# Turned products of an inverse transform in DRAM: laid out by rows, written in pieces, read as one run per partition

## The chip, the cores and the metric

The kernel runs on one core of a Trainium2 chip. The core has five engines that run their own instruction streams side by side: TensorE (matmuls; PE in the profile, with its weight loads as PEld), VectorE (DVE), ScalarE (ACT), GpSimd (POOL) and SyncE (SP), which here only issues DMAs. 16 DMA engines move data between DRAM and the on-chip memory SBUF, whose first dimension is 128 partitions. Matmul results go to PSUM and are copied out by ScalarE or VectorE. The metric is the time of one execution on the device, in microseconds (us); lower is better.

## The reference

An input x of 2048 steps by 512 channels goes through two branches, which a gate mixes:

```python
x = A_u
g = _sigmoid((x * gate_w).sum(-1, keepdims=True))
a = _A_ref(x, ...)      # state space model as a long convolution
b = _B_ref(x, ...)      # linear attention, 32 heads of 16
return g * a + (1 - g) * b
```

The change touches the end of branch A. There a kernel K of 2048 taps is made for each channel, and the convolution is done by Fourier transforms of length 4096:

```python
K = jnp.einsum("dn,dnl,dn->dl", Cc, P, dB).real
Kf = rfft(pad(K));  Uf = rfft(pad(u))
Yf = Uf * Kf
y = irfft(Yf)[:L] + u * Dskip
```

## The kernel before

The program is one long list of nodes (class `Plan`), each with its engine; a string `ORDER`, written out by hand, sets the order in which all are issued, and so each engine's order and SyncE's queue. An engine runs its instructions strictly in that order. DMAs share eight lanes (`"ln": 8`), so a ninth waits for an earlier one to land.

The first part (to about 100 us) makes tables, transforms u and writes its spectrum to DRAM (`XUd`). The second part works through 16 units of 32 channels: `kgen` makes the taps K of a unit (products `A` and `R` on VectorE at L1097, L1108, L1115, L1119, matmuls `kps` at L179) and their first transform step (`psA`, L186). When the channels of a group are ready, `transform` finishes the convolution for them. The groups are: Q = 0, 1 and 2 with nd = 128 channels each (units 0 to 3, 4 to 7, 8 to 11), and in Q = 3 one group of nd = 64 (units 12, 13), one of nd = 32 (unit 14) and a last one of nd = 32 (unit 15). Branch B's attention runs between these on the same engines.

Inside `transform`, for `ns` frequency rows r at a time (8, 16 or 32 for nd = 128, 64 or 32):

- `load` (L1182, for Q = 3 L1184) brings the spectrum of u from DRAM into a tile XUX, of which there are three; it is a pair of DMAs of 256 KB. `psB` (L192) makes the spectrum of K, a copy takes it to `XK`, and VectorE multiplies the two: tile `t` (L1229; for the nd = 32 groups L1232, in two halves).
- `fi` (L1261) multiplies with the table TI as weights: the first step of the inverse transform. Its 128 outputs stand on the partitions, numbered by t (32), h (2) and a (2); the free dimension holds (r, d), d the channel. ScalarE copies them to a tile `Zr` (two buffers).
- The second step contracts over a and r and needs them on the partitions, with t on the free dimension. The products are turned through DRAM: `fw` (L1274) writes each `Zr` to a DRAM tensor `Zd`, four times for nd = 128, twice for nd = 64, once for nd = 32; `fr` (L1283) reads `Zd` back into a tile ZT of 128 partitions, 64 partitions (one h, called `th`) with each of two DMAs. A reading waits until all writings of its group have landed.
- `py` (L1339) does the second step from ZT with the table TJ: `psy`. For nd = 128 it comes in two instalments, the first with the first reading's half, the second with the other's. `ou` (L1361, L1364) scales with the gate and stores the result, which is then written to the output.

The last group (unit 15, `far` false) does not go through DRAM: `iz` (L1295) takes `t` as weights and TI as the moving operand, one t half and one a at a time.

ZT shares one buffer (tag `ax`) with the attention's factors `ax`. These go through DRAM too: `aw` (L895) writes them to `apd` as 64 KB, and `ar` (L902) reads them back as four DMAs of 256 KB. Each reading repeats 8 rows of DRAM for 16 partitions each: its DRAM side is `.unsqueeze(1).to_broadcast([8, 16, 1024])` against 128 partitions of SBUF. VectorE multiplies with them at L909.

The table TI itself is made at about 7 us by two sines on ScalarE and three small operations of VectorE (L299 to L301).

Of the kernel before, what the change touches and what calls it, by code (L numbers as in the profile page):

```python
# [13 lines left out]
BF16 = mybir.dt.bfloat16  # L14
# [1041 lines left out]
def plan_conv(P, nc, g, psum, r):  # L1056

    fc, act, at, xT = g.fc, g.act, g.at, g.xT
# [6 lines left out]
    def evict2(name, get, deps, ps):  # L1065
        out = []
        for k in range(2):
            out.append(P.add(("ACT", "DVE"), name, lambda k=k: P.copy(*get(k)), [ps] + deps[k] + out, drop=(["psum"] if k else [])))
        return out
# [119 lines left out]
    def transform(XA, ready, Q, off, nd, far, Ls, last, co=0, free=True, split=False):  # L1189

        F = Bag()
        ng, ns, nj, nt = nd // 2, 1024 // nd, min(16, 1024 // nd) if far else 8, min(32, 2048 // nd)
# [4 lines left out]
        ov = g.out2d[:, 128 * (Q - pair) + lo:128 * Q + off + nd].rearrange("(q j c) d -> c q j d", q=32, j=16, c=4)  # L1197
        bS = xT[:, :, Q, :]
        if far:
            F.Zd = g.dram.tile([32, 4, 32, nd], BF16, name=f"Zd{Q}_{off}")  # L1200
        tn, zn, rn, wn = [], [], [], []
        for r0 in range(0, 32, ns):
            box = Bag()
# [44 lines left out]
            x = evict2("XK", xk, [[], []], b) if split else [evict("XK", xk, [b])]  # L1248
# [8 lines left out]
            def fi(box=box):  # L1257
                box.ps = psum([128, 2, 512], "psz")
                for hb in range(2):
                    for k in range(2):  # L1260
                        nc.tensor.matmul(box.ps[:, hb, :], lhsT=fc.TI[:, k].rearrange("p t h a -> p (t h a)"), rhs=box.t[:, k, 512 * hb:512 * hb + 512],  # L1261
                                         start=(k == 0), stop=(k == 1))
                box.t = None

# [6 lines left out]
                return o, i  # L1271

            def fw(r0=r0, box=box):
                nc.sync.dma_start(out=F.Zd[:, :, r0:r0 + ns, :].rearrange("t x r d -> (t x) r d"), in_=box.Z[:])  # L1274
                box.Z = None
            z = P.add("PE", "psz", fi, [tn[-1]] + ([z] if r0 else []), take=[psq, "Zr"], drop=(["r8"] if (r0 + ns) % nt == 0 else []), rw=("TI", ""))
            zn.append(evict("Zr", fe, [z] + zn[-1:]))
            wn.append(P.dma("zw", 0.45, 2.0, fw, [zn[-1]], drop=["Zr"], move=0.9))

        def fr(th):  # L1280
            if th == 0:
                F.Z = g.fpool.tile([128, 4096], BF16, name="ZT", tag="ax", bufs=g.P.k["ax"])[:, 0:32 * nd].rearrange("p (t d) -> p t d", d=nd)
            nc.sync.dma_start(out=F.Z[64 * th:64 * th + 64], in_=F.Zd[:, 2 * th:2 * th + 2].rearrange("t x r d -> (x r) t d"))  # L1283
        for th in range(2 if far else 0):
            rn.append(P.dma("zr", 0.6, 2.0, lambda th=th: fr(th), wn + [n.issue for n in rn[-1:]], take=(["ax"] if th == 0 else []), move=max(1.2, 2.8 * nd / 128 + 0.1)))
        box = Bag()
# [25 lines left out]
        for j0 in range(0, 16, nj):  # L1312
            box = Bag()
# [81 lines left out]
    for h in range(6):  # L1395
        for u in (2 * h, 2 * h + 1):
            if u in g.PHASES and u:
                phase(range(u, g.PHASES[u]))
        if h % 2 == 0:
            XA = Bag()  # L1400
            XA.nd, XA.off, XA.drop, done = 128, 0, True, []
        done = done + kgen((2 * h, 2 * h + 1), XA, h % 2 == 0)
        if h % 2:
            transform(XA, done, h // 2, 0, 128, True, [load(h // 2, p) for p in range(4)], False)
# [7 lines left out]
    for k, (units, far) in enumerate(g.LAST):  # L1412
        XA = Bag()
        XA.nd, XA.off, XA.first = 32 * len(units), 32 * (units[0] - 12), first
        XA.drop = units[-1] == 15
        done = kgen(units, XA, True, units in g.SPLIT)
        first = XA.first
        end = units[-1] == 15
        off = 32 * (units[0] - 12)
        transform(XA, done, 3, off, XA.nd, far, L[off // 64 * 2:off // 64 * 2 + 2], end, off % 64, units[-1] % 2 == 1, units in g.SPLIT)  # L1420


def full_kernel(tc, A_u, A_A_re, A_A_im, A_B_re, A_B_im, A_C_re, A_C_im, A_log_dt, A_Dskip,
                B_x, B_wqkv, B_w_phi, B_wo, gate_w, out):
    nc = tc.nc
# [3 lines left out]
    def pool(ctx, name, bufs=1, **kw):  # L1429
        return ctx.enter_context(tc.tile_pool(name=name, bufs=bufs, reuse_waits="tile", **kw))  # L1430
    with ExitStack() as ctx:
        g, fc, at = Bag(), Bag(), Bag()
# [6 lines left out]
        persist = pool(ctx, "persist")  # L1439
# [6 lines left out]
        g.zrow = persist.tile([128, 4, 128], F32, name="zrow")  # L1446
        fc.W1 = persist.tile([128, 2, 32, 4], BF16, name="W1")
        fc.TB = persist.tile([128, 97, 64], BF16, name="TB")
        fc.TI = persist.tile([128, 2, 32, 2, 2], BF16, name="TI")
        fc.TJ = persist.tile([128, 64, 32], BF16, name="TJ")  # L1450
        g.CX = [persist.tile([128, 3072], BF16, name=f"Ctab{h}") for h in range(2)]
        g.C = [c[:].rearrange("p (o a c) -> p o a c", o=3, a=4) for c in g.CX]
# [111 lines left out]
        r = keys_and_spectrum(P, nc, g, psum)  # L1564
# [7 lines left out]
@with_exitstack  # L1572
def kernel(
    ctx: ExitStack,
    tc: tile.TileContext,
    A_u: bass.AP,
    A_A_re: bass.AP,
    A_A_im: bass.AP,
    A_B_re: bass.AP,
    A_B_im: bass.AP,  # L1580
    A_C_re: bass.AP,
    A_C_im: bass.AP,
    A_log_dt: bass.AP,
    A_Dskip: bass.AP,
    B_x: bass.AP,
    B_wqkv: bass.AP,
    B_w_phi: bass.AP,
    B_wo: bass.AP,
    gate_w: bass.AP,
    out: bass.AP,  # L1590
):
    full_kernel(tc, A_u, A_A_re, A_A_im, A_B_re, A_B_im, A_C_re, A_C_im, A_log_dt, A_Dskip,
                B_x, B_wqkv, B_w_phi, B_wo, gate_w, out)
# [30 lines left out]
```

## Time and profile before

| what | value |
|---|---|
| time, median of 3 runs (lowest, highest) | 264.5 us (263.61, 264.85) |
| the profiled execution's own time | 264.49 us |
| its span, first to last instruction | 262.7 us |
| VectorE busy, ScalarE busy | 231.0 us, 221.1 us |
| TensorE busy, mean granted clock | 195.3 us, 0.927 |
| packets of SyncE's DMA queue, as a share of 16 engines' span | 54.5% |
| bytes moved by all DMAs | 35.93 MB |

The span is 1.8 us shorter than the time of the same execution. Busy times are sums over one engine; they overlap with those of the others. In the timeline a row gives the start in us, the duration, engine, line, operation, tiles (out<-in), shape and count; in square brackets stands how long the engine had been idle and what released it. Rows of SyncE (SPq) are the issuing alone: the data moves afterwards. A row of a DMA queue (q1 is SyncE's) gives packets, MB and the share of the time of 16 engines in the window that was asked for.

The kernel's chain of work that ended last consists of VectorE for 35%, ScalarE 27%, TensorE 18%, DMA 8%.

### The profile page before, as it was taken

Reading aid. Unit: us, or ns where it says so; the run is one execution under the profiler, and the core shown is the slowest. Engines: PE = TensorE matmul, PEld = TensorE weight load, DVE = VectorE, ACT = ScalarE, POOL = GpSimd, SP = SyncE. Lnnn points to the kernel's source line nnn. Section 1 sums busy time; section 2 is a strip of 40 time slices with the busy share of each in tenths; the row PEclk is TensorE's granted clock in tenths of the full one; section 3 lists DMA queues with packets and bytes.
Section 4 is the critical chain, followed back from the end, with each engine's and each line's share of the span. In section 5 each row is a group of like instructions: output and inputs, shape, how many; then the busy total and the mean of one; then the engine's idle time right before and its main releaser. Section 6 shows DMA issues by size and latency. Waiting matters only on the chain.

```text
span 262.7 us, 10078 instructions
## 1 busy us (share of the span) xinstructions
PE 195.3 (74%) x4512; PEld 132.4 (50%) x4512; DVE 231.0 (88%) x314; ACT 221.1 (84%) x305; POOL 11.7 (4%) x22
## 2 busy tenths in 40 slices
PE   0386899999945569888468656989978598998750
PEld 0275665755633234355346244575765376774630
DVE  6799799898799998999999999989999999975440
ACT  7976998888899999999999998999999997765000
POOL 4750000000000000000000000000000000000000
PEclk9997999999999597999899999899999999999655
DMA  6799000352630576602240536258945697979784
GB/s 196 140 192 214 4 4 0 99 154 62 202 95 24 178 220 182 206 4 86 101 150 15 162 130 201 67 152 160 226 148 199 175 195 229 166 214 161 176 102 82
DMA packets 67547, 35.93 MB, mean 137 GB/s; under 512 B 46000, under 2 KB 62000, under 8 KB 67504
## 3 DMA queue, kind: packets, MB, share of 16 engines
q1 hardware_dynamic: 66448, 35.16, 54.5%
q8 instruction: 35, 0.57, 1.0%
q10 hardware_dynamic: 1056, 0.13, 0.3%
q14 instruction: 8, 0.07, 0.1%
HBM read 22.17 MB, written 13.11 MB: 134 GB/s over the span
## 4 chain that ended last, share of the span: by engine, by line
DVE 35%; ACT 27%; PE 18%; DMA 8%; issue 8%; SPq 1%; DVEq 0%; ACTq 0%
DVE A L1097 7%; DMA XUX<-XUd 4%; DVE t L1229 3%; PE pk L705 3%; ACT Eq L68 3%; ACT XA L145 2%; ACT xst L145 2%; ACT E L68 2%; DMA ax<-apd 2%; DVE XAu L147 2%; DVE R L1119 2%; ACT cs L68 2%; DVE R L1115 2%; ACT Zr L145 2%; DMA pz<-pt 2%
## 5 line engine op out<-in xcount | busy, mean ns | idle before, releaser
L1097 DVE TENSOR_TENSOR A<-Ctab,Dtab 128x2048 bf16<-128x2048 bf16 x32 | 38.7, 1219 | 0.2
L68 ACT ACTIVATE cs<-args 128x1024 bf16<-128x1024 f32 x32 | 30.9, 1063 | 0.0
L179 PE MATMUL kps<-R,A 128*32 128x64 bf16 x1536 | 18.1, 204 | 8.0 <-DVE A L1097 1.8
L179 PEld LDWEIGHTS <-A 128*32 128x32 bf16 x1536 | 16.3, 118 | 12.0 <-issue 5.6
L1115 DVE TENSOR_TENSOR R<-E,cs 128x2048 bf16<-128x2048 bf16 x16 | 19.5, 1220 | 1.6 <-ACT E L68 1.5
L1119 DVE TENSOR_TENSOR R<-E,cs 128x2048 bf16<-128x2048 bf16 x16 | 19.5, 1217 | 0.0
L68 ACT ACTIVATE Ek<-pk 128x512 bf16<-128x512 f32 x32 | 16.7, 602 | 2.5 <-PE pk L705 2.5
L1261 PE MATMUL psz<-t,TI 128*128 128x512 bf16 x60 | 15.6, 388 | 2.8 <-DVE t L1229 1.2
L1229 DVE TENSOR_TENSOR t<-XUX,XK 128x2048 bf16<-128x2048 bf16 x14 | 17.0, 1218 | 0.4 <-ACT XK L145 0.4
L145 ACT CAST XA<-psA 128x1024 bf16<-128x1024 f32 x15 | 15.1, 1042 | 2.6 <-PE psA L186 2.6
L68 ACT ACTIVATE E<-args 128x1024 bf16<-128x1024 f32 x16 | 16.8, 1057 | 0.2 <-PE args L1041 0.2
L145 ACT CAST Zr<-psz 128x1024 bf16<-128x1024 f32 x15 | 15.4, 1027 | 1.6 <-ACT xT L977 0.7
L68 ACT ACTIVATE Eq<-pq 128x512 bf16<-128x512 f32 (+1 forms) x28 | 16.6, 692 | 0.1
L145 ACT CAST XK<-psB 128x1024 bf16<-128x1024 f32 x15 | 15.4, 1035 | 1.6 <-PE psB L192 1.5
L753 PE MATMUL vp<-WW,xT 128*128 128x512 bf16 x64 | 16.7, 395 | 0.0
L839 PE MATMUL pq<-xT,Wqp 128*128 128x512 bf16 x64 | 16.1, 388 | 0.4 <-ACT Eq L68 0.4
L612 PE MATMUL psB<-XAu,TB 64*128 64x128 bf16 x256 | 9.7, 222 | 8.2 <-ACT xst L145 6.4
L705 PE MATMUL pk<-WW,xT 128*128 128x512 bf16 x64 | 15.2, 380 | 0.0
L186 PE MATMUL psA<-W,KD 128*64 128x128 bf16 x256 | 10.0, 221 | 5.3 <-ACT cs L68 3.1
L192 PE MATMUL psB<-XA,TB 128*128 128x128 bf16 (+2 forms) x192 | 10.1, 200 | 4.5 <-ACT XK L145 1.4
L612 PEld LDWEIGHTS <-TB 64*128 64x128 bf16 x256 | 7.8, 97 | 11.0 <-issue 11.0
L65 ACT ACT_TABLE_LOAD x10 | 12.8, 1283 | 0.1
(210 smaller groups left out, 497.2 us busy)
## 6 DMA issues: line engine op xcount, KB each, us to landing
XUX<-XUd SPq DMA_DIRECT2D x32, 256.0 KB, 5.3
XUd<-xst SPq DMA_DIRECT2D x8, 512.0 KB, 3.1
ax<-apd SPq DMA_DIRECT2D x16, 256.0 KB
Zd<-Zr SPq DMA_DIRECT2D x15, 256.0 KB, 2.4
ZT<-Zd SPq DMA_DIRECT2D x6, 512.0 KB
UD<-in_A_u_dram SPq DMA_DIRECT2D x16, 128.0 KB, 4.5
XUd<-xst SPq DMA_DIRECT2D x8, 256.0 KB
wqk<-in_B_wqkv_dram SPq DMA_DIRECT2D x1, 1024.0 KB
```

The lines of the kernel that those rows point to most:

```text
L68: return self.nc.scalar.activation(**kw)
L145: self.nc.scalar.copy(out=o, in_=i)
L179: nc.tensor.matmul(kps[32 * dj:32 * dj + 32, g4, e, :], lhsT=A[:, d // 4, 32 * ka:32 * ka + 32, d % 4], rhs=R[:, kr, d, :], start=(i == 0) ...
L612: nc.tensor.matmul(box.ps[:, c2, sl, :], lhsT=fc.TB[rows, b0:b0 + 2].rearrange("p a b -> p (a b)"), rhs=X.t[rows, k, r0 + sl].rearrange("p ...
L705: nc.tensor.matmul(box.ps[:], lhsT=xT[:, st, kt, :], rhs=g.WW[:, kt, :], start=(kt == 0), stop=(kt == 3))
L753: nc.tensor.matmul(box.ps[:], lhsT=xT[:, st, kt, :], rhs=g.WW[:, 4 + kt, :], start=(kt == 0), stop=(kt == 3))
L839: nc.tensor.matmul(box.ps[:, m - m0, :] if late else box.ps[:], lhsT=g.Wqp[:, kt, 128 * m:128 * m + 128], rhs=xT[:, 4 * b:4 * b + 4, kt, : ...
L1097: nc.vector.tensor_tensor(out=c.A[:, :, 64 * k:64 * k + 64, :].rearrange("p q (x b) l -> p x b q l", b=8), in0=cf.unsqueeze(2).to_broadcas ...
L1115: nc.vector.tensor_tensor(out=c.R[:, :, :, 32:64], in0=t.E[:, 1].unsqueeze(1).to_broadcast([128, 2, 32, 32]), in1=t.cs[:], op=ALU.mult)
L1119: nc.vector.tensor_tensor(out=c.R[:, :, :, 0:32], in0=t.E[:, 0].unsqueeze(1).to_broadcast([128, 2, 32, 32]), in1=t.cs[:, ::-1, :, ::-1], o ...
L1229: nc.vector.tensor_tensor(out=box.t, in0=Ls[r0 // ns].X[:], in1=box.XK[:].unsqueeze(1).to_broadcast([128, 2, 1024]), op=ALU.mult)
L1261: nc.tensor.matmul(box.ps[:, hb, :], lhsT=fc.TI[:, k].rearrange("p t h a -> p (t h a)"), rhs=box.t[:, k, 512 * hb:512 * hb + 512], start=( ...
```

## The change

The order of the products on the partitions becomes (h, a, t) instead of (t, h, a): the tile behind TI is laid out as [k, h, a, t], and `fc.TI` becomes a view of it with the old order of its dimensions, through which it is made and through which L1295 reads it. With x = (h, a), partition 32·x + t now holds what partition 4·t + x held.

For nd = 128 and 64 (`byrow`) `Zd` is now indexed [r, x, t, d] instead of [t, x, r, d]. A writing puts, for each partition, `ns` pieces of nd elements to places 128·nd elements apart (before: one run of 1024 elements). A reading takes for each of 64 partitions one run of 32·nd elements (before: 32 pieces of nd elements). For nd = 32 `Zd` keeps its layout; the writing names its partitions as x, then t, and the reading is unchanged.

| | before: DRAM side | after: DRAM side |
|---|---|---|
| writing, nd = 128 (256 KB) | 128 runs of 2 KB | 128 partitions with 8 pieces of 256 B |
| writing, nd = 64 (256 KB) | 128 runs of 2 KB | 128 partitions with 16 pieces of 128 B |
| writing, nd = 32 (256 KB) | 128 runs of 2 KB, evenly spaced | 4 (x) with 32 (t) runs of 2 KB |
| reading, nd = 128 (512 KB) | 64 evenly spaced rows with 32 pieces of 256 B | 2 (x) with 32 (r) runs of 8 KB |
| reading, nd = 64 (256 KB) | 64 evenly spaced rows with 32 pieces of 128 B | 2 (x) with 32 (r) runs of 4 KB |

In the readings after the change a step of x is 32·nd elements and a step of r is 128·nd.

```diff
         if far:
+            byrow = nd > 32
             F.Zd = g.dram.tile([32, 4, 32, nd], BF16, name=f"Zd{Q}_{off}")
...
-                        nc.tensor.matmul(box.ps[:, hb, :], lhsT=fc.TI[:, k].rearrange("p t h a -> p (t h a)"), rhs=box.t[:, k, 512 * hb:512 * hb + 512],
+                        nc.tensor.matmul(box.ps[:, hb, :], lhsT=fc.TIp[:, k].rearrange("p h a t -> p (h a t)"), rhs=box.t[:, k, 512 * hb:512 * hb + 512],
...
             def fw(r0=r0, box=box):
-                nc.sync.dma_start(out=F.Zd[:, :, r0:r0 + ns, :].rearrange("t x r d -> (t x) r d"), in_=box.Z[:])
+                if byrow:
+                    nc.sync.dma_start(out=F.Zd[r0:r0 + ns].rearrange("r x t d -> (x t) r d"), in_=box.Z[:])
+                else:
+                    nc.sync.dma_start(out=F.Zd[:, :, r0:r0 + ns, :].rearrange("t x r d -> x t (r d)"), in_=box.Z[:].rearrange("p r d -> p (r d)"))
                 box.Z = None
...
-            nc.sync.dma_start(out=F.Z[64 * th:64 * th + 64], in_=F.Zd[:, 2 * th:2 * th + 2].rearrange("t x r d -> (x r) t d"))
+            if byrow:
+                nc.sync.dma_start(out=F.Z[64 * th:64 * th + 64], in_=F.Zd[:, 2 * th:2 * th + 2].rearrange("r x t d -> x r t d"))
+            else:
+                nc.sync.dma_start(out=F.Z[64 * th:64 * th + 64], in_=F.Zd[:, 2 * th:2 * th + 2].rearrange("t x r d -> (x r) t d"))
...
-        fc.TI = persist.tile([128, 2, 32, 2, 2], BF16, name="TI")
+        fc.TIp = persist.tile([128, 2, 2, 2, 32], BF16, name="TI")
+        fc.TI = fc.TIp[:].rearrange("p k h a t -> p k t h a")
```

The order of issue is the same string as before.

## The prediction

> **What bounds the kernel now.** I read the page first (busy shares), then VectorE's and TensorE's timeline around the readings of Zd, SyncE's timeline from 150 us on, and last the packets of three short windows.
>
> ```profile
> PE 195.3 (74%) x4512; PEld 132.4 (50%) x4512; DVE 231.0 (88%) x314; ACT 221.1 (84%) x305; POOL 11.7 (4%) x22
> Zd<-Zr SPq DMA_DIRECT2D x15, 256.0 KB, 2.4
> ```
>
> VectorE works 231.0 of 262.7 us, so until the tail a DMA matters only when it comes so late that VectorE or TensorE stands still. The points where they use what comes from DRAM are these (VectorE and TensorE, in order of time):
>
> ```profile
> 201.78 1.22 DVE L909 TENSOR_TENSOR Eq<-Eq,ax 128x2048 bf16<-128x2048 bf16 x1
> 213.76 0.63 PE L1339 MATMUL psy<-ZT,TJ 64*32 64x128 bf16 x32
> 215.95 1.21 DVE L1364 TENSOR_TENSOR xT<-psy,gT 128x1024 bf16<-128x1024 f32 x1
> 221.72 0.63 PE L1339 MATMUL psy<-ZT,TJ 64*32 64x128 bf16 x32
> 225.09 1.22 DVE L1097 TENSOR_TENSOR A<-Ctab,Dtab 128x2048 bf16<-128x2048 bf16 x1
> 232.97 0.63 PE L1339 MATMUL psy<-ZT,TJ 64*32 64x128 bf16 x32
> 233.65 0.69 DVE L1361 TENSOR_TENSOR xT<-psy,gT 128x512 bf16<-128x512 f32 x1 [0.46 <-PE psy L1339]
> 239.48 0.69 DVE L1232 TENSOR_TENSOR t<-XUX,XK 128x1024 bf16<-128x1024 bf16 x1 [0.73 <-DMA XUX<-XUd]
> 243.88 0.68 PE L1339 MATMUL psy<-ZT,TJ 64*32 64x64 bf16 x64
> 246.34 3.64 PE L1295 MATMUL psz<-TI,t 128*32 128x64 bf16 x128 [1.78 <-DVE t L1232]
> 253.99 0.77 PE L1339 MATMUL psy<-ZT,TJ 64*32 64x32 bf16 x64
> ```
>
> No `psy` waits for ZT by a DMA's name: today the readings are hidden. Only 239.48 waits for a DMA, a load of XUX. And this is SyncE's queue, all on one ring:
>
> ```profile
> 153.10 2.46 SPq L902 DMA_DIRECT2D ax<-apd  x4
> ...
> 174.29 0.63 SPq L1283 DMA_DIRECT2D ZT<-Zd  x1
> 179.27 0.87 SPq L1182 DMA_DIRECT2D XUX<-XUd  x2
> 180.19 0.61 SPq L1283 DMA_DIRECT2D ZT<-Zd  x1
> 182.15 3.03 SPq L1182 DMA_DIRECT2D XUX<-XUd  x2
> 186.06 0.33 SPq L1274 DMA_DIRECT2D Zd<-Zr  x1
> 187.29 0.93 SPq L1182 DMA_DIRECT2D XUX<-XUd  x2
> 188.98 0.33 SPq L1274 DMA_DIRECT2D Zd<-Zr  x1
> 190.47 0.33 SPq L895 DMA_DIRECT2D apd<-apm  x1
> ...
> 195.34 2.51 SPq L902 DMA_DIRECT2D ax<-apd  x4
> ...
> 206.98 0.62 SPq L1283 DMA_DIRECT2D ZT<-Zd  x1
> 210.13 1.62 SPq L1274 DMA_DIRECT2D Zd<-Zr  x2
> 211.79 0.61 SPq L1283 DMA_DIRECT2D ZT<-Zd  x1
> 212.45 2.83 SPq L1184 DMA_DIRECT2D XUX<-XUd  x2
> 217.77 1.91 SPq L1274 DMA_DIRECT2D Zd<-Zr  x2
> 219.77 1.37 SPq L1184 DMA_DIRECT2D XUX<-XUd  x2
> 222.49 2.46 SPq L1283 DMA_DIRECT2D ZT<-Zd  x2
> 230.20 1.73 SPq L1274 DMA_DIRECT2D Zd<-Zr  x2
> 231.98 1.87 SPq L1184 DMA_DIRECT2D XUX<-XUd  x4
> 247.84 2.12 SPq L1283 DMA_DIRECT2D ZT<-Zd  x2
> ```
>
> **How many DMA engines a transfer gets.** The window from 155 to 159 us holds data of the four `ax` readings of 153.10 and little else; beside it stand one of XUX loads with 1 KB rows (148 to 150), one of 256 B writings (59 to 60) and one of 128 B writings (254.5 to 257), each with packets, MB and the share of 16 engines:
>
> ```profile
> q1 hardware_dynamic: 369, 0.71, 50.5%
> XUX<-XUd SPq DMA_DIRECT2D x2, 256.0 KB, 7.0
> ...
> q1 hardware_dynamic: 579, 0.56, 89.5%
> ...
> q1 hardware_dynamic: 819, 0.22, 95.5%
> ...
> q1 hardware_dynamic: 1831, 0.23, 66.8%
> ```
>
> With four transfers outstanding, only 50.5% of 16 engines work: eight. If each `ax` reading had eight engines of its own, two would fill all 16; so all four use the same eight. L902 reads `.to_broadcast([8, 16, 1024])`: eight outermost rows on the DRAM side against 128 partitions. The XUX loads, whose two sides both start with 128, fill 16 (89.5%). So I read: the engines of a transfer are as many as divide the outermost counts of both sides, and always the same ones. The XUX loads issued behind `ax` took 7.0 us to land: what is queued later waits on those engines.
>
> The Trainium skill, "DMA: Bandwidth & Descriptors", section "Why a DMA increments its semaphore by 16 and not by 1", states this rule for all shapes: the largest number up to 16 that divides both sides' slowest counts, taken from the lowest engine on. By it the new readings get two engines and the nd = 32 writing four, which speaks against the change; the half share above agrees with it, and no run here shows two yet.
>
> **The change, part by part.** *Readings of Zd (nd 128 and 64).* Before, `(x r)` were 64 evenly spaced rows: one count of 64. After, in `r x t d -> x r t d` a step of x is 32·nd elements and one of r 128·nd, so they do not merge: the DRAM side starts with 2, against 64 partitions. I take two engines. Each moves 32 rows of 8 KB. Price of a row: 155 to 159 gives 0.505·16·4.0 = 32.3 us of engine time for 0.71 MB, 22 B/ns, 93 ns per 2 KB; 148 to 150 gives 0.895·16·2.0 = 28.6 us for 0.56 MB, 52 ns per 1 KB. The step, 41 ns a KB, makes an 8 KB row 93 + 6·41 = 339 ns and a reading **10.8 us** (nd = 64, 4 KB rows, 175 ns: 5.6). Bounds: at 22 B/ns 11.9; at 41 ns a KB throughout 10.5.
> *Writings (nd 128 and 64).* Both sides keep 128 outermost: 16 engines. 1024 pieces of 256 B, 64 an engine, at 0.955·16·1000/819 = 18.7 ns: 1.2 us, before 8 rows of 2 KB, 0.74. nd = 64: 128 pieces of 128 B at 0.668·16·2500/1831 = 14.6 ns: 1.9 us.
> *The nd = 32 writing.* `x t (r d)` starts with 4: four engines, 32 rows of 2 KB each, 3.0 us instead of 0.74. Its readings stay.
> *Others on an engine:* a pair of XUX loads 2·16·52 = 1.7 us with 1 KB rows (L1182), 2·8·93 = 1.5 with 2 KB rows (L1184). Around its 0.74 us of data a writing takes 2.4 to land: I put 0.8 ahead and 0.9 behind.
> *TI.* L1261's weights stay a run of 128. The three small operations that make TI, and L1295, get other steps; this counts 0 here (L1295 is in the rivals; what covers the small ones is their size).
>
> The sum follows the two engines through their queue (times of before; S is the shift of VectorE):
> - Q = 0: ZT 174.29, data 175.1 to 185.9. XUX to 187.6. Second ZT to **198.4**, and `psy` behind it. Then XUX 200.1, Zd 201.3, XUX 203.0, Zd 204.2, `apd` (a quarter of a writing) 204.4, landed 205.3. `ax` needs it: issued at 205.3, not 195.34. Two `ax` on eight engines, 2·16·93 ns = 3.0, with 1.7 around and the issue land at about 210.3; L909 stood at 201.78: **S = 8.5**. SyncE is blocked behind `ax` all that time.
> - Q = 1: ZT 206.98 + 8.5 = 215.5, data 216.3 to 227.1, landed 228.0, `psy` to 228.6. L1364 (215.95): **S = 12.7**. On the engines two Zd (229.5), second ZT to 240.3, landed 241.2. `psy` was due at 221.72 + 12.7 = 234.4, 6.8 late; about 1 of this lies in TensorE's own gaps ahead of L1097 (225.09): **S = 18.5**.
> - Q = 2: behind that reading XUX, two Zd, XUX (1.5 + 2.4 + 1.5) to 245.7; Zd landed at 245.1, so ZT goes out then, not at 222.49 + 18.5 = 241.0. Two readings to 256.7 and 267.5, landed 268.4; `psy` to 269.0, L1361 (233.65): **S = 35.4**.
> - Q = 3: two Zd of nd = 64 (271.3), two XUX pairs (274.3), landed 275.2: L1232 (239.48) S = 35.7. The nd = 64 readings to 279.9 and 285.5, landed 286.4; `psy` due at 243.88 + 35.7 = 279.6, 6.8 late, of which the 1.78 ahead of L1295 are covered: **S = 40.7**. The nd = 32 writing to 288.5, landed 289.4, and its reading out 41.6 after 247.84; the `psy` of 253.99 had little slack: **S = 41**.
>
> Behind that the tail is as before. The profiled execution took 264.49 us (span 262.7 and 1.8 around it), the median of the runs is 264.5: 264.5 + 41 = 305.5, **306 us**.
>
> Seven readings in a row carry the sum: at 11.9 each it is 313, at 10.5 304. TensorE's granted clock (third from the end of a window's row) is lower where it idles:
>
> ```profile
> 254.00:257.00 3.00, 0.76 (x65) 0.57 (x64) 0.70 (x2) 0.00 (x0) 0.00 (x0) 0.50 0.67 94
> ```
>
> Five waits of 5 to 13 us may leave it at half speed for a while each time; I put up to 2 us for each, 10 in all. Against that, work that I let stand still may run on in parts, 1 to 2 us at each of the five points, and as no trace shows a row of 8 KB its price may lie below 10.5. That makes 290 to 324 for this case.
>
> **Rivals.** *(a) All 16 engines read.* The half share at 155 might come from `ax`'s repeated rows, not from its eight. Then a reading has four 8 KB rows an engine, 1.4 us, everything above is hidden, and one cost is left: L1232 waits for XUX loads queued behind the nd = 64 writings, whose second takes 1.9 instead of 0.74. VectorE idles for them already, so 1.1 us go straight to the end: **265.6**. For it: nothing but the untested shape; against it, XUX repeats no row and loses none of its engines.
> *(b) Faster.* With 16 engines as in (a), TI's t lies in a run where L1295 reads it in steps of 8 B. L1295 takes 3.64 us for 128, 28 ns each, on the path to the end; the same form in `kps` takes 18.1/1536 us, 12 ns:
>
> ```profile
> L179 PE MATMUL kps<-R,A 128*32 128x64 bf16 x1536 | 18.1, 204 | 8.0 <-DVE A L1097 1.8 <-issue 1.7 <-ACT XA L145 1.5
> ```
>
> If the steps are the cause, 128·16 ns = 2.1 us go; where the XUX delay stays under 0.8, as when the first writing is done before the second is issued, the kernel comes out at **262.8**. Against it: L1295's weights and its output are stepped too and stay so. The Trainium skill, "SBUF — State Buffer", section "Door 1: The DMA port swizzle", says that bf16 may be read in steps of up to 8 elements for free and that PSUM suffers from any gap; TI's step is 4, so by this nothing is gained and (b) falls to (a). No row here parts the three.
> *(c) Two engines, but another pair for each reading.* Then readings do not wait for one another. Q = 0: `apd` behind one reading, S about 1.7. Q = 1: ZT 208.7, landed 221.2 (0.8 + 10.8 + 0.9), `psy` to 221.8, L1364 (215.95) S = 5.9. Q = 2: ZT 228.4, landed 240.9, 4 to 5 later than its first `psy`, which runs some 3 us ahead of 232.97, is due; S = 10.7: **275**. Against it: the four `ax` shared the same eight.
>
> **How the numbers follow.** Forecast 0.84, (c) 0.04, (a) and its like 0.09, (b) 0.03. 290 to 324 holds the forecast's case 95 times in 100, which is 8 in 10 of all; the others lie below, and reaching to them would leave out less than 2 in 10. About 0.5% (1.3 us) is what can be told from no change. Slower: 0.84 + 0.04 + 0.04 of (a); same 0.05 of (a); faster 0.03.
>
> **What would show it.** Right: ZT readings of over 10 us to landing; a DMA share near 2/16 in stretches after 190 us; L1339 waiting for `ZT<-Zd`, L1232 and L909 for their loads; SyncE waiting at L902 for `apd`; four engines for the nd = 32 writing. Wrong: ZT landing in 3 to 4 us and a share near 1 in its window (then (a) or (b), parted by L1295's duration); or two readings landing together (c).

## The result, and the profile after

The changed kernel takes 324.9 us (median of 4 runs, 320.05 to 327.41) where the kernel before takes 264.1 on the same chip. Two of the four runs, the profiled one among them, took over 1.5% longer than the fastest; the ratio, 1.219 with a 95% interval of 1.205 to 1.233, goes by the other two (mean 321.9). The forecast was 306, range 290 to 324: the direction and the mechanism came out, and the size was short, by 16 us for these two and by 19 for the median, which lies 0.9 above the range. The profiled execution of the changed kernel took 327.4 us, with a span of 325.6 against 262.7 before: 62.9 us more, where the forecast had S = 41.

New lines of code move the numbers. The old L1229, L1232, L1283, L1295, L1339, L1361 and L1364 are L1230, L1233, L1288 (rows) or L1290 (nd = 32), L1302, L1346, L1368 and L1371 now. The old L1274 is L1276 (rows) or L1278 (nd = 32).

From the page of the changed kernel, the busy shares, the chain that ended last by engine, and the median landing of the writings:

```profile
PE 208.0 (64%) x4492; PEld 141.6 (43%) x4512; DVE 232.6 (71%) x314; ACT 221.6 (68%) x305; POOL 11.7 (4%) x22
...
DMA 36%; DVE 20%; ACT 19%; PE 15%; issue 6%; POOL 1%; SPq 1%; DVEq 0%; ACTq 0%; POOLq 0%
...
Zd<-Zr SPq DMA_DIRECT2D x15, 256.0 KB, 16.3
```

VectorE does the same work (232.6 us against 231.0) in a longer span; the chain that ended last, 35% VectorE and 8% DMA before, now follows DMAs for 36%, and a writing of Zd, 2.4 us from issue to landing before, takes 16.3. The waits view of the changed kernel (engine and line, what it waited for: us in total, times, longest) names the place:

```profile
PE psy L1346 <- DMA ZT<-Zd: 46.4, 8, 12.7
...
DVE xT L1368 <- PE psy L1346: 21.3, 1, 21.3
DVE xT L1371 <- PE psy L1346: 12.9, 2, 10.7
...
DVE t L1230 <- DMA XUX<-XUd: 7.6, 1, 7.6
...
DVE Eq L909 <- DMA ax<-apd: 4.5, 2, 4.2
```

Before, no psy waited for ZT. Now eight do. The same points in VectorE's and TensorE's timeline that the forecast used, in the changed kernel:

```profile
216.69 1.23 DVE L909 TENSOR_TENSOR Eq<-Eq,ax 128x2048 bf16<-128x2048 bf16 x1 [4.17 <-DMA ax<-apd]
242.24 1.23 DVE L1371 TENSOR_TENSOR xT<-psy,gT 128x1024 bf16<-128x1024 f32 x1 [10.75 <-PE psy L1346]
261.16 1.23 DVE L1097 TENSOR_TENSOR A<-Ctab,Dtab 128x2048 bf16<-128x2048 bf16 x1 [7.86 <-PE kps L179]
291.04 0.69 DVE L1368 TENSOR_TENSOR xT<-psy,gT 128x512 bf16<-128x512 f32 x1 [21.27 <-PE psy L1346]
296.36 0.69 DVE L1233 TENSOR_TENSOR t<-XUX,XK 128x1024 bf16<-128x1024 bf16 x1 [0.63 <-DMA XUX<-XUd]
308.09 4.05 PE L1302 MATMUL psz<-TI,t 128*32 128x64 bf16 x128
316.50 0.40 PE L1346 MATMUL psy<-ZT,TJ 64*32 64x32 bf16 x32
```

Each less its own time of before gives the shift S at that point, to be read beside the forecast's:

| point | before, us | after, us | S measured | S forecast |
|---|---|---|---|---|
| Q = 0, L909 | 201.78 | 216.69 | 14.9 | 8.5 |
| Q = 1, first half (L1364, now L1371) | 215.95 | 242.24 | 26.3 | 12.7 |
| Q = 1, behind the second half (L1097) | 225.09 | 261.16 | 36.1 | 18.5 |
| Q = 2 (L1361, now L1368) | 233.65 | 291.04 | 57.4 | 35.4 |
| nd = 64, L1232 (now L1233) | 239.48 | 296.36 | 56.9 | 35.7 |
| psz (L1295, now L1302) | 246.34 | 308.09 | 61.8 | 40.7 |
| psy of nd = 32 | 253.99 | 316.50 | 62.5 | 41 |

The steps are where the forecast put them: at Q = 0, at both halves of Q = 1, the largest at Q = 2, nothing at L1232, some 5 at nd = 64. Each of the first four is larger than forecast. SyncE's timeline shows why all else is late with the readings:

```profile
177.40 0.53 SPq L1288 DMA_DIRECT2D ZT<-Zd  x1
...
182.88 0.53 SPq L1288 DMA_DIRECT2D ZT<-Zd  x1
...
206.70 1.46 SPq L895 DMA_DIRECT2D apd<-apm  x1
...
211.20 2.51 SPq L902 DMA_DIRECT2D ax<-apd  x4
...
222.19 0.53 SPq L1288 DMA_DIRECT2D ZT<-Zd  x1
224.56 11.31 SPq L1276 DMA_DIRECT2D Zd<-Zr  x2
235.91 4.97 SPq L1288 DMA_DIRECT2D ZT<-Zd  x1
...
260.24 1.05 SPq L1288 DMA_DIRECT2D ZT<-Zd  x2
266.73 22.85 SPq L1276 DMA_DIRECT2D Zd<-Zr  x2
```

`ax` goes out at 211.20 instead of 195.34, and issuing a pair of writings takes 11 and 23 us; the second of each pair alone stands on the queue for 8.8 and 21.4. The first reading itself is issued at 177.40 instead of 174.29, which no reading can have caused: 3.1 us of this execution's 62.9 were there before any reading (e4 below, with the same readings, issued it at 174.55).

Now the rows. In the DMA view of the changed kernel (packets, MB and share of 16 engines; then the issues), here first from 199 to 205 us and then from 230 to 236:

```profile
q1 hardware_dynamic: 52, 0.32, 12.8%
```

```profile
q1 hardware_dynamic: 23, 0.19, 12.4%
issues: line engine op xcount, KB each, median us to landing
ZT<-Zd SPq DMA_DIRECT2D x1, 512.0 KB
```

12.5% is two engines of 16, both busy all the time. The semaphore of such a reading (the counter through which a DMA tells that its data have landed) says the same in the trace: it is raised once at the issue and then twice; that of the nd = 32 writing once and then four times; those of the readings before sixteen times, all as data land. In the second window the two engines moved 23 rows: 0.124 x 96,000 ns / 23 = 518 ns a row, 31 GB/s. In the first, 0.32 MB in the same 6 us. Taken packet by packet, the 8 KB rows of the six readings of nd = 128 lie in two groups, 208 of 384 under 350 ns (202 of them from 309 to 325) and 116 over 500 (87 of them from 600 to 670):

```
reading        Q0 first  Q0 second  Q1 first  Q1 second  Q2 first  Q2 second   all
mean ns a row       452        316       523        446       519        327   431
```

### The profile page after: what moved, and what is told of

It reads as the page before. It is cut to its first block, busy times and chain, and to the rows that moved or that the text cites. A ratio compares the mean times of both kernels' runs of the same rounds, so it can differ in the third digit from the quotient of the medians.

```text
span 325.6 us, 10058 instructions
## 1 busy us (share of the span) xinstructions
PE 208.0 (64%) x4492; PEld 141.6 (43%) x4512; DVE 232.6 (71%) x314; ACT 221.6 (68%) x305; POOL 11.7 (4%) x22
## 4 chain that ended last, share of the span: by engine, by line
DMA 36%; DVE 20%; ACT 19%; PE 15%; issue 6%; POOL 1%; SPq 1%; DVEq 0%; ACTq 0%; POOLq 0%
DMA ZT<-Zd 22%; DMA Zd<-Zr 14%; ACT cs L68 3%; DVE A L1097 3%; PE pk L705 2%; ACT xst L145 2%; PE kps L179 2%; DVE XAu L147 2%; DVE tgv L265 1%; PE vp L753 1%; ACT E L68 1%; ACT Ek L68 1%; ACT XA L145 1%; PE psz L1302 1%; PE kvp L770 1%
## 5 line engine op out<-in xcount | busy, mean ns | idle before, releaser
L1097 DVE TENSOR_TENSOR A<-Ctab,Dtab 128x2048 bf16<-128x2048 bf16 x32 | 38.7, 1220 | 8.5 <-PE kps L179 8.4
L1346 PE MATMUL psy<-ZT,TJ 64*32 64x128 bf16 (+2 forms) x320 | 7.2, 246 | 46.4 <-DMA ZT<-Zd 46.4
L145 ACT CAST XK<-psB 128x1024 bf16<-128x1024 f32 x15 | 15.2, 1021 | 23.2 <-PE psB L192 23.1
L1346 PEld LDWEIGHTS <-TJ 64*32 64x32 bf16 x320 | 5.8, 114 | 48.3 <-issue 48.0
L179 PE MATMUL kps<-R,A 128*32 128x64 bf16 x1536 | 19.4, 212 | 9.4 <-issue 4.9
L68 ACT ACTIVATE E<-args 128x1024 bf16<-128x1024 f32 x16 | 16.8, 1056 | 12.6 <-PE args L1041 12.6
L179 PEld LDWEIGHTS <-A 128*32 128x32 bf16 x1536 | 17.3, 119 | 14.7 <-issue 9.0
L1230 DVE TENSOR_TENSOR t<-XUX,XK 128x2048 bf16<-128x2048 bf16 x14 | 17.0, 1219 | 8.6 <-DMA XUX<-XUd 7.6
L1262 PE MATMUL psz<-t,TI 128*128 128x512 bf16 x53 | 17.0, 434 | 4.7 <-DVE t L1230 1.8
L186 PE MATMUL psA<-W,KD 128*64 128x128 bf16 x256 | 11.5, 241 | 9.1 <-ACT apm L68 5.0
L1368 DVE TENSOR_TENSOR xT<-psy,gT 128x512 bf16<-128x512 f32 x3 | 2.1, 686 | 21.3 <-PE psy L1346 21.3
L753 PE MATMUL vp<-WW,xT 128*128 128x512 bf16 x58 | 15.7, 393 | 0.8 <-issue 0.7
L186 PEld LDWEIGHTS <-KD 128*64 128x64 bf16 x256 | 9.4, 122 | 12.9 <-issue 10.1
## 6 DMA issues: line engine op xcount, KB each, us to landing
Zd<-Zr SPq DMA_DIRECT2D x15, 256.0 KB, 16.3
```

The costliest lines, as they stand in the source:

```text
L68: return self.nc.scalar.activation(**kw)
L145: self.nc.scalar.copy(out=o, in_=i)
L179: nc.tensor.matmul(kps[32 * dj:32 * dj + 32, g4, e, :], lhsT=A[:, d // 4, 32 * ka:32 * ka + 32, d % 4], rhs=R[:, kr, d, :], start=(i == 0) ...
L186: nc.tensor.matmul(ps[64 * ri:64 * ri + 64], lhsT=lhsT, rhs=fc.W1[:, ri].rearrange("p r d -> p (r d)"), start=True, stop=True, tile_positi ...
L753: nc.tensor.matmul(box.ps[:], lhsT=xT[:, st, kt, :], rhs=g.WW[:, 4 + kt, :], start=(kt == 0), stop=(kt == 3))
L1097: nc.vector.tensor_tensor(out=c.A[:, :, 64 * k:64 * k + 64, :].rearrange("p q (x b) l -> p x b q l", b=8), in0=cf.unsqueeze(2).to_broadcas ...
```

## The experiments

All are variants of the kernel before or of the changed kernel; only what is shown or said here differs. In the cuts of code, `...` stands for lines left out. Unless said otherwise, `ratio` is to the kernel before on the same chip.

**e1: the reading cut by x.** The layout stays; only the number of engines should change.

```diff
-                nc.sync.dma_start(out=F.Z[64 * th:64 * th + 64], in_=F.Zd[:, 2 * th:2 * th + 2].rearrange("r x t d -> x r t d"))
+                for i in range(2):
+                    nc.sync.dma_start(out=F.Z[64 * th + 32 * i:64 * th + 32 * i + 32], in_=F.Zd[:, 2 * th + i])
...
-                    nc.sync.dma_start(out=F.Zd[:, :, r0:r0 + ns, :].rearrange("t x r d -> x t (r d)"), in_=box.Z[:].rearrange("p r d -> p (r d)"))
+                    for x in range(4):
+                        nc.sync.dma_start(out=F.Zd[:, x, r0:r0 + ns, :], in_=box.Z[32 * x:32 * x + 32])
```

> Theory E (the readings are slow because their DRAM side starts with 2 rows of x, which leaves them two DMA engines; the writing of nd = 32 has four for the same reason): with each reading cut in two by x, both halves starting with 32 rows on both sides, and that writing cut in four, every half spreads over 16 engines: an 8 KB row costs 0.31 to 0.34 us and two of them stand on an engine, so a half's data take under 1 us. No psy waits for ZT any more, VectorE's shift S is 0 to 1.5 us (the 128 B pieces of nd = 64 ahead of the XUX loads), and the kernel takes 264 to 266 us. Rival L (the layout costs by itself: 8 KB rows at a pitch of 32 KB, or pieces of 256 B and 128 B on the writing side): nothing of that is changed here, so the time stays above 300 us. The stepped read of TI is as in the changed kernel; were it a gain of 2.1 us at the old L1295, 262.8 would come out.

Measured 266.5 us, ratio 1.009 (1.005 to 1.013). Cutting each reading in two, and the one nd = 32 writing in four, gives back 55 of the 58 us (321.9 against 264.1), with every row, piece and byte where the change put them. The semaphore of each half is now raised sixteen times as data land, and with the halves of Q = 2 under way (224 to 230 us) the DMA view of e1 has

```profile
q1 hardware_dynamic: 183, 0.95, 68.7%
```

So the loss is in the number of engines, not in the layout. 266.5 lies just above theory E's 264 to 266; the waits view of the kernel before and then that of e1 say where the rest is:

```profile
DVE t L1232 <- DMA XUX<-XUd: 3.1, 2, 2.3
```

```profile
DVE t L1233 <- DMA XUX<-XUd: 5.8, 2, 2.9
```

No psy waits for ZT; L1233 waits 5.8 us for XUX, against 3.1 before. SyncE's timeline of e1 shows the loads behind the two writings of nd = 64:

```profile
230.34 1.79 SPq L1276 DMA_DIRECT2D Zd<-Zr  x2
232.23 4.05 SPq L1184 DMA_DIRECT2D XUX<-XUd  x4
```

Four issues take 4.05 us, where before they took 1.87; ahead of them stand the pieces of 128 B.

**e2 and its control: the kernel before, its readings cut 62 + 2 and 48 + 16.** This is the other direction: the old layout, with another number of rows in a DMA.

```diff
-            nc.sync.dma_start(out=F.Z[64 * th:64 * th + 64], in_=F.Zd[:, 2 * th:2 * th + 2].rearrange("t x r d -> (x r) t d"))
+            src = F.Zd[:, 2 * th:2 * th + 2].rearrange("t x r d -> (x r) t d")
+            for lo_, hi_ in ((0, 62), (62, 64)):
+                nc.sync.dma_start(out=F.Z[64 * th + lo_:64 * th + hi_], in_=src[lo_:hi_])
```

> The kernel before, layout and pieces untouched, each reading only cut into 62 and 2 of its 64 rows. Theory E: the largest number up to 16 that divides 62 is 2, so the reading falls to two engines with 31 rows of 32 pieces each; at the 18.7 ns that a 256 B piece cost in the writings that is 992 x 18.7 ns = 18.6 us per reading (nd = 64, 14.6 ns: 14.5 us), 8 us more than the 10.8 of the changed kernel's forecast, seven times in a row: 340 to 380 us. Rival L (it is the layout, not the number of engines): the layout is that of before, so 264 to 267 us.

> The control of the cut into 62 and 2: the same kernel before, each reading cut into 48 and 16 rows, both of which 16 divides. Theory E: 16 engines for both, one DMA more per reading on SyncE: 264 to 266 us. If a second DMA in a reading is itself what costs, this one is as slow as 62 and 2.

62 + 2 takes 375.8 us (1 run), 48 + 16 takes 267.2 (ratio 1.010, 1.003 to 1.018). The same bytes in the same pieces, in as many DMAs, cost 109 us more; what differs is that 16 divides 48 and 16, but not 62. From 199 to 206 us the DMA view of e2 shows the pieces of one reading alone:

```profile
q1 hardware_dynamic: 774, 0.20, 16.8%
issues: line engine op xcount, KB each, median us to landing
ZT<-Zd SPq DMA_DIRECT2D x1, 16.0 KB
```

0.20 MB in 7 us. The trace shows the semaphore of such a reading raised once at the issue and then twice, when the data of two engines have landed; that the share is 16.8 and not 12.5% I put down to packets of one engine that overlap in the records. A second DMA in a reading costs little by itself: the control lies 1% above before, a little over its expectation of 264 to 266.

**e3: the new order of TI, the old layout for all transforms.** So all fifteen writings have a DRAM side that starts with 4.

```diff
-            byrow = nd > 32
+            byrow = False
```

> The changed kernel with the new order of TI, but the old layout of Zd for all transforms: readings as before (64 even rows, 16 engines), all fifteen writings on four engines (their DRAM side starts with 4). Theory E: a writing's data take 32 rows of 2 KB x 93 ns = 3.0 us instead of 0.74, lands in about 5 us instead of 2.4, and loads of XUX queued behind it are up to 2.3 us later; readings are still hidden: 265 to 270 us, L1232 waiting for XUX more than before. Rival L: without the row layout, and pieces of 256 B again on the reading side, 264 to 265. If the new order of TI costs or gains anything, it shows in the duration of the 128 matmuls of the old L1295 (3.64 us before).

Measured 282.4 us, ratio 1.068 (1.061 to 1.074): slower than theory E said, by 12 us at its upper end. The waits view of e3:

```profile
DVE t L1233 <- DMA XUX<-XUd: 5.1, 2, 3.8
...
DVE t L1230 <- DMA XUX<-XUd: 3.3, 1, 3.3
PE psy L1346 <- DMA ZT<-Zd: 2.8, 2, 1.5
DVE Eq L909 <- DMA ax<-apd: 2.6, 3, 1.5
ACT Zr L145 <- DMA Zd<-Zr: 2.2, 2, 2.1
```

I had charged only the loads of XUX. Readings, `ax` and the buffers of Zr wait as well. The writings do have four engines: their semaphores are raised once at the issue and then four times, and from 174 to 176 us, with two of them on their way, 25.3% of the 16 engines work. That these four hold up everything on the queue that also needs them is my reading of the waits. TI's order is not the cause: e1 has it too and takes 266.5 us, and the 128 matmuls of psz take as long as before (shown with the prediction's points below).

**e7: one engine.** Each half of a reading is cut again, into 31 and 1 rows.

```diff
-                nc.sync.dma_start(out=F.Z[64 * th:64 * th + 64], in_=F.Zd[:, 2 * th:2 * th + 2].rearrange("r x t d -> x r t d"))
+                for i in range(2):
+                    for lo_, hi_ in ((0, 31), (31, 32)):
+                        nc.sync.dma_start(out=F.Z[64 * th + 32 * i + lo_:64 * th + 32 * i + hi_], in_=F.Zd[lo_:hi_, 2 * th + i])
```

> The changed kernel, each reading of nd = 128 and 64 cut by x and each half into 31 and 1 rows: 31 and 1 leave one engine by the rule of the largest divisor, so all 64 rows of a reading go through one engine and no other engine reads rows at the time. Theory S or P (620 ns comes from two engines in step): every row takes about 313 ns, a reading 64 x 0.313 = 20.0 us, and at 9.2 us more than the forecast's 10.8 for seven readings in a row the kernel takes 306 + 64 = 370 us (355 to 385). Rival M (the memory or the queue slows single rows, whatever the other engine does): rows of 620 ns stay among them, 25 us or more a reading, over 400 us. Should the engine count be no matter of 31 and 1, the time would be 270 or below.

Measured 372.8 us (1 run), 370 expected. From 188 to 194 us, the DMA view of e7:

```profile
q1 hardware_dynamic: 19, 0.16, 6.2%
```

6.2% is one engine of 16, and 0.062 x 96,000 / 19 = 313 ns a row. Of all 384 rows 365 took under 350 ns and 10 over 500, where the two engines of the changed kernel had 116. So the slow rows come with the second engine. One engine alone moved 0.16 MB in 6 us, while both together moved 0.19 in the changed kernel's slow stretch: there the second engine added hardly anything. Counts 62 and 31 with their two engines and one are also what the Trainium skill says of the largest common divisor up to 16 of the two sides' outermost counts ("DMA: Bandwidth & Descriptors", section "Why a DMA increments its semaphore by 16 and not by 1"); these runs agree, with 16.8% and 6.2% of the engines, and with two raises and one behind that at the issue.

**e4 and e10: where do the two engines meet?** In the changed kernel's slow stretches three rows of four are slow on each engine, and the rows that the two read side by side are 8 KB apart in DRAM. e4 changes the pitch from r to r, e10 the distance from x to x (its writing is cut in four by x).

First e4's edit, then e10's (the views of Zd then leave out what was added):

```diff
-            F.Zd = g.dram.tile([32, 4, 32, nd], BF16, name=f"Zd{Q}_{off}")
+            F.Zd = g.dram.tile([32, 5 if byrow else 4, 32, nd], BF16, name=f"Zd{Q}_{off}")
```

```diff
-            F.Zd = g.dram.tile([32, 4, 32, nd], BF16, name=f"Zd{Q}_{off}")
+            F.Zd = g.dram.tile([32, 4, 33 if byrow else 32, nd], BF16, name=f"Zd{Q}_{off}")
```

> The changed kernel with 40 KB instead of 32 KB from one row r of Zd to the next (nd = 128), all else the same, two engines included. In the changed kernel the 8 KB rows of a reading took 313 ns or about 620 ns, and in the slow stretches three rows of four were slow, while both engines started their rows within 0.2 us of one another. Theory P (the pitch: two engines in step meet in the memory because rows of x are 8 KB apart at a pitch of 32 KB, every fourth row excepted): with 40 KB the rows go to 313 to 340 ns, a reading to 10 us, and the kernel to 300 to 308 us, the forecast with the row price that it was made with. Theory S (two engines in step collide whatever the pitch is): some rows stay at 620 ns, 318 to 328 us.

> The changed kernel with 33 instead of 32 rows t stored for each x, so that the two rows that the two engines read side by side lie 8.25 KB apart instead of 8 KB (33 KB from r to r); the writing, whose partitions no longer merge over x, is cut in four by x, 32 partitions and 16 engines each. The readings keep two engines. Theory B (rows whose distance is a power of two meet in the same part of the memory while the engines are in step): nearly all rows take 313 to 340 ns, as on one engine alone, a reading 10 to 11 us, and the time is 302 to 312 us (the forecast's 306, with some 3 us more for 42 further issues). Theory S (two engines in step disturb each other wherever their rows lie): near a third of the rows stays at about 620 ns, a mean near 430, and the time is 318 to 330 us.

e4 took 323.8 and 329.7 us (2 runs) and e10 334.8 (2 runs; ratio 1.265, 1.258 to 1.273). The mean row was 428 ns in e4, with 114 rows of 384 over 500 ns, and 435 in e10, with 130. Either may change and the rows stay as slow as they were: theories P and B fall, S holds. e10 lies 5 us above S's range; its 42 further issues stand on the same queue. The changed kernel's trace adds when rows are slow. For the four readings of Q = 1 and 2 the packets part into two unbroken sequences, one for each engine. At the middle of 71 rows the other engine was within half a row of the same place: these took 584 ns in the mean, 51 of them over 500. At the middle of 66 it was three rows or more ahead or behind: these took 322, none over 500. So, as far as these four show, a slow stretch ends where one engine is some three rows ahead. What the two share is not settled; moving their targets in SBUF apart, which would be the next question, was not tried.

**e6: the readings from GpSimd's queue.**

```diff
-                nc.sync.dma_start(out=F.Z[64 * th:64 * th + 64], in_=F.Zd[:, 2 * th:2 * th + 2].rearrange("r x t d -> x r t d"))
+                nc.gpsimd.dma_start(out=F.Z[64 * th:64 * th + 64], in_=F.Zd[:, 2 * th:2 * th + 2].rearrange("r x t d -> x r t d"))
```

> The changed kernel, its readings of ZT for nd = 128 and 64 issued from GpSimd's queue instead of SyncE's; the same two engines. Theory Q (part of the loss is what stands behind a reading in its queue: the loads of XUX, the writings of Zd, apd): the waits at L909 and L1230 for apd and XUX go, the shift of Q = 0 (8.5 by the forecast) with them; what is left is psy waiting for readings that are late themselves: by the forecast's own sum without that shift some 20 at Q = 2 and 25 at Q = 3 at 10.8 us a reading (290 us), up to 308 us at the 13 us that readings took in the changed kernel. Rival (what costs is the length of the seven readings alone): 318 to 327 us as before the move, since the same two engines carry them.

Measured 307.8 us (2 runs; ratio 1.164, 1.154 to 1.174), the upper end of theory Q. The waits view of e6, and the DMA view from 186 to 192 us:

```profile
PE psy L1346 <- DMA ZT<-Zd: 33.3, 4, 12.5
...
DVE t L1230 <- DMA XUX<-XUd: 13.6, 1, 13.6
```

```profile
q0 software_dynamic: 42, 0.34, 23.5%
```

L909's wait is gone, as expected, but L1230 waits longer for XUX, not less, and the expectation's premise was wrong: 23.5% is nearly four engines, so here the two readings of Q = 0 ran side by side on two each. (By the same section of the Trainium skill, a queue of this kind hands each transfer the next engines in turn; this one run agrees, with its 23.5%.) Four engines moved 0.34 MB in 6 us, 537 ns a row: as much as the changed kernel's two in a clear stretch. So e6 does not part the queue from the engines cleanly. It shows that even another pair for each reading, the forecast's rival (c), leaves the kernel 16% slower.

**e9 and e5: what e1 still lost.** e9 lays out by rows only nd = 128; nd = 64 and 32 are as in the kernel before, with a second copy of TI in the old order. e5 is e1 with the writings of nd = 64 issued from GpSimd's queue.

First e9's edit, beside e1's readings, then e5's:

```diff
-            byrow = nd > 32
+            byrow = nd > 64
...
-                    nc.sync.dma_start(out=F.Zd[:, :, r0:r0 + ns, :].rearrange("t x r d -> x t (r d)"), in_=box.Z[:].rearrange("p r d -> p (r d)"))
+                    nc.sync.dma_start(out=F.Zd[:, :, r0:r0 + ns, :].rearrange("t x r d -> (t x) r d"), in_=box.Z[:])
```

```diff
-                    nc.sync.dma_start(out=F.Zd[r0:r0 + ns].rearrange("r x t d -> (x t) r d"), in_=box.Z[:])
+                    (nc.gpsimd if nd == 64 else nc.sync).dma_start(out=F.Zd[r0:r0 + ns].rearrange("r x t d -> (x t) r d"), in_=box.Z[:])
```

> The row layout for nd = 128 alone, its readings cut by x as in e1; nd = 64 and 32 write and read as in the kernel before (a second copy of TI in the old order serves them, one small VectorE operation at the start). Theory W (what e1 still loses to before are the 128 B pieces of nd = 64 ahead of the XUX loads): L1233's wait for XUX goes back from 5.8 to about 3 us and the time to 264 to 265 us, a ratio to before within 0.4%. Rival (the loss of e1 lies in the cut readings and the 256 B pieces of nd = 128): 266 to 267 us, 0.7 to 1%. A gain on before is expected by neither: VectorE waits for none of the nd = 128 readings there.

> The cut by x (e1) with the two writings of nd = 64 issued from GpSimd's queue, idle at that time. In e1 the issue of the XUX load behind them stood 2.62 us, and L1233 waited 5.8 us for XUX in all, against 3.1 before. Theory W (these 2.4 us of e1 come from the 4096 pieces of 128 B standing ahead of the XUX loads in SyncE's queue): the wait at L1233 falls to 3 us or less and the time to 263 to 265 us, no slower than before. Rival (the loss of e1 is in the further DMAs that the cut adds, or in the engines which the pieces take in any queue): 266 to 267 us.

e9 takes 264.6 us, ratio 1.003 (0.999 to 1.006), and its wait for XUX is down to 2.1 us:

```profile
DVE t L1234 <- DMA XUX<-XUd: 2.1, 2, 1.3
PE psy L1348 <- DMA ZT<-Zd: 1.2, 1, 1.2
```

By these ratios most of e1's 0.9% came from what it does to nd = 64 and 32 (the pieces of 128 B, and the cut readings and writing, which these runs do not part), and with 16 engines the row layout of nd = 128 costs and gains nothing that can be measured. e5 takes 266.1, ratio 1.006 (1.003 to 1.009). Its wait for XUX is gone, as theory W had it, and yet the time lies in the rival's range: psy waits 3.9 us for ZT instead, since from that queue the first of the two writings takes 4.8 us from issue to landing, against 3.3 in e1. The wait has only moved, and e5 can't be told from e1.

**e8: the kernel before, with only the two writings of nd = 64 on GpSimd's queue.** The one variant that might have beaten before.

> The kernel before, with only the two writings of nd = 64 issued from GpSimd's queue, as in e5. If the loads of XUX at L1232 wait because they are issued behind those writings on SyncE, its 3.1 us of waiting shrink; the writings' later landing from that queue may hold the nd = 64 readings instead, as psy waited 3.9 us in e5. First theory (the waits only change places): 263.5 to 266 us. Second theory (the XUX wait was on the path and the readings have slack for the later landing): 261 to 263 us.

263.8 us, ratio 0.998 (0.995 to 1.002): the wait of 3.1 us for XUX is gone, 1.6 us of psy for ZT have come, and the time has not changed by anything that can be measured. No variant here beats the kernel before.

**e11: the change for nd = 64 and 32 alone.**

```diff
-            byrow = nd > 32
+            byrow = nd == 64
```

nd = 128 writes and reads as in the kernel before.

> The change for nd = 64 and 32 alone (the readings of nd = 64 on two engines, the writing of nd = 32 on four), nd = 128 as in the kernel before, with the copy of TI of e9. The forecast's terms for these steps were 5.0 us (S from 35.7 to 40.7) and 0.3 us (to 41). Theory T (the terms hold by themselves, with the 0.7 to 2.4 us that the 128 B pieces cost at L1233 in e1 on top): 270 to 272 us. Rival (the two nd = 64 readings are late only because the queue was late already, and by themselves lie in the slack around L1232): 266 to 268 us.

271.7 us, ratio 1.034 (1.028 to 1.039), inside theory T. TensorE's timeline of e11:

```profile
250.73 3.39 PE L1306 MATMUL psz<-TI,t 128*32 128x64 bf16 x128
...
259.73 0.41 PE L1350 MATMUL psy<-ZT,TJ 64*32 64x32 bf16 x32 [1.51 <-DMA ZT<-Zd]
261.68 0.40 PE L1350 MATMUL psy<-ZT,TJ 64*32 64x32 bf16 x32 [1.54 <-DMA ZT<-Zd]
```

psz is 4.4 us later than in before (250.73 against 246.34): the forecast's 5.0 for the readings of nd = 64. Behind it another 2.7 come up to the end (span 269.8, 7.1 over before), with both readings of nd = 32 late behind their four-engine writing: here 0.3 was too little. The second L1234 stands at 239.78 here, 0.3 after its time in before (239.48), though the four issues of XUX behind the same pieces of 128 B took 4.08 us again: how e1 loses its last 2.4 us is therefore not settled, only that most of it lies with nd = 64 and 32 (e9).

## Why the prediction was right, and where it was short

**The number of engines: right.** The new readings have two (12.4 to 12.8% of 16), and it is the shape of the DMA that decides: e1 changes the count by one more DMA a reading and gives the loss back; e2, with one more DMA a reading too, makes a larger loss in the old layout, and its control none. Rival (a), 16 engines in one DMA, is refuted by the changed kernel itself.

**The readings of nd = 64: right.** Their 4 KB rows took 174 ns in e11, 175 forecast; 4.4 us measured for a term of 5.0.

**Everything behind a reading is held: right.** From 170 us on the chain that ended last consists of readings of Zd for 43.8% and of its writings for 28.2%: the second reading of Q = 0, the first of Q = 1, then a writing and a reading behind it each of Q = 2 and nd = 64. `ax` is not on it. L909 did wait 4.2 us for `ax`, as forecast, but at Q = 0 the chain goes from the second reading through `psy` and on over ScalarE and TensorE, a second path that the forecast's sum does not follow. By it the first reading of Q = 1 goes out 15.2 us later than before (222.19 against 206.98), about as late as L909 is (14.9).

**The price of an 8 KB row: the mis-sized term.** 339 ns, and 10.8 us a reading, hold where a row is undisturbed (313 in e7 and in the changed kernel's clear stretches). The mean was 431, and the bounds (10.5 to 11.9 us a reading) had no place for it: they asked how a row's price grows with its size, and put at nothing that the two engines delay one another. From the table of means, 32 rows an engine at (mean - 339): +3.6, -0.7, +5.9, +3.4, +5.8 and -0.4 us, together 17.6. With the 3.1 us by which this execution was late before the first reading, 41 + 17.6 + 3.1 = 61.7, and 62.9 was measured. It fits step by step as well: at the first four points of the table the shift grew by 11.8 (without the 3.1), 11.4, 9.8 and 21.3 us; the forecast's steps with the rows put right are 11.4, 10.1, 9.2 and 22.3. e4 checks the same sum in another execution: its rows averaged 466, 316, 520, 506, 447 and 315 ns, 17.1 us over the forecast; 41 + 17.1 = 58.1, and its span was 59.2 over before. That 321.9 still lies inside the range is luck in part: the upper end had 10 us of room for a slower clock, and it was the rows that used it.

**The clock, and the work that runs on while psy waits: little.** TensorE was busy 208.0 us instead of 195.3, at a mean granted clock of 0.835 instead of 0.927, but with the rows put right 1.2 us are left for both allowances together. The forecast read that the clock is lower where TensorE idles. Two windows of the changed kernel (first us and TensorE's busy time, third from the end the clock) show that it need not be so:

```profile
199.00:205.00 6.00, 4.25 (x102) 3.18 (x102) 5.66 (x6) 5.21 (x7) 0.00 (x0) 0.55 0.15 57
230.00:236.00 6.00, 0.24 (x5) 0.16 (x3) 1.49 (x2) 0.18 (x1) 0.00 (x0) 0.92 0.12 31
```

In the first, where TensorE works 4.25 of 6 us, the clock is 0.55; in the second, where psy waits for ZT and it works 0.24, the clock is 0.92.

**The four-engine writing of nd = 32: too small.** 0.3 forecast, 2.7 alone (e11); in the changed kernel 62.9 - 61.8 = 1.1. It did have four engines, but from issue to landing it took 8.4 us in e11 and 7.6 in the changed kernel, where the forecast had 3.0 of data and 0.9 behind them.

**L1295 and TI, rival (b): nothing.** From the instruction groups of the kernel before and then of the changed kernel (busy us, mean ns):

```profile
L1295 PE MATMUL psz<-TI,t 128*32 128x64 bf16 x128 | 3.6, 347 | 1.8 <-DVE t L1232 1.8
```

```profile
L1302 PE MATMUL psz<-TI,t 128*32 128x64 bf16 x128 | 3.9, 345 | 0.1
```

The granted clock was 0.50 in both, and t lying in a run gained nothing. The bf16 step of 4 was free, as the Trainium skill has it ("SBUF — State Buffer", section "Door 1: The DMA port swizzle"). What made these matmuls dear is for the most part the clock and not the steps: in e5, with the new order and a clock of 1.00 at this point, the same 128 took 2.2 us, 17 ns each; at 0.56 they took 3.4 (e11, new order) and at 0.60 3.3 (e8, order of before). No run shows the order of before at 1.00.

**Rival (c), another pair for each reading: not what SyncE's queue does,** and from the queue that does, 307.8 and not 275 (e6): in the window shown a row costs 537 ns instead of 313 when two readings run at once, which the rival's sum did not have.

## What to carry to other kernels

Before a DMA's layout is made friendlier (fewer, longer runs), look at the outermost count that is left on each side after merging: a "2" there turned 16 engines into 2, and a reading that no engine had waited for into one of 10 to 17 us (32 rows an engine at 316 to 523 ns). If a stride no longer merges, cut the DMA at that dimension; one further issue a reading (some 0.4 us each) bought back most of the 55 us here. And ask first whether the transfer is waited for at all: with the engines restored (e9), the tidier reading was worth nothing, because no engine had waited for the old one.

## What the runs showed of the hardware that was not expected

- Two engines that read 8 KB rows at once delay one another in long stretches: rows of 313 ns become 600 to 670, three of four, and the pair moves 31 GB/s (0.19 MB in 6 us) where one engine alone moves 26. In other stretches both take 313 to 320; in the four readings whose packets can be told apart by engine, no row was slow where the two were three rows or more apart. Neither the pitch (32, 33, 40 KB) nor the distance of the two rows (8, 8.25 KB) mattered. Four engines in e6 had 537 ns a row in the window shown, and 16 in e1 had 551 in the mean of all rows. What is shared stays open.
- A DMA issue can stand on its queue while many pieces are ahead of it. In e2 the two issues of a reading, of 62 rows and of 2, held SyncE for most of that reading (us from the start, us, engine, line):

```profile
174.48 18.79 SPq L1285 DMA_DIRECT2D ZT<-Zd  x2
```
